# Clock-keeping products left out, projection units regrouped, and four weight splits moved from GpSimd to VectorE in an attention and two-layer kernel

## The chip, the cores and the metric

The kernel runs on one core of one Trainium2 chip. The metric is device time in microseconds, the median of several runs. The profile is one execution of the same program, with times counted from the start of its span. TensorE appears in it as PE (matmuls) and PEld (weight loads), VectorE as DVE, ScalarE as ACT, GpSimd as POOL and SyncE, which issues every transfer here, as SP.

## The reference, cut to what matters

```python
def sm_attn(qq, kk, vv):                     # softmax(scale * q k^T) v
    ...
p_packed = sm_attn(p, k, v)                  # 32 packed queries read 576 keys, per head
out = sm_attn(q, p_packed, p_packed)         # 576 queries read the 32 packed rows
x = out.transpose(0, 2, 1, 3).reshape(4608, 512)
xn = x / sqrt(mean(x * x) + 1e-6) * rms_g
g, val = xn @ w_gate, xn @ w_val             # 512 x 1536 each
x = (g * sigmoid(g) * val) @ w_out           # 1536 x 512
h = x @ w_in                                 # 512 x 2048
out = (h * cos(h)) @ w2_out                  # 2048 x 512
```

There are 8 batches with 8 heads of 64 columns, 576 tokens in each batch, float32 throughout. Some weights arrive in 64-bit form and are narrowed in the kernel (lines L134 to L150).

## The kernel before, in words

The program has four stretches, one behind the other.

**The prologue** (loop over `i`, 18 rounds, two to a batch) computes the packed attention for four heads at a time. A round transposes keys on PE (`u_kt`, tile `kp`, copied out by ACT as `kT`), multiplies packed queries with them (`u_s1`, tile `s`; the packed queries stand in a tile padded with zeros to 128 columns), takes the exponential on ACT (`u_e`), transposes it (`u_et`, tile `et`), and multiplies it with the values (`u_pp`, tile `pp`, 24 small products). Ahead of each group of transposes and of each third of the value products stands a call of `keep_hot`, one 128 x 288 product of a constant tile `hot` with itself, whose result is overwritten or not read. It has no use but to occupy PE. Along with this, rounds load and narrow the weights of the first layer (`w_prep`), and from round 4 on they do pieces of the second attention of batch 0 (`bg0_step`: tiles `qtp`, `sp`, `atp`, `xp`).

From round 10 on a round also does one or two **projection units** (`project`): the packed outputs times a block of the gate or value weights, four products into two PSUM tiles `mps`, which ACT and DVE copy out to `ev` (lines L528, L529); a store to DRAM is queued. In the prologue the tag `mm` has two PSUM buffers, so that a second unit, or a piece of attention with the same tag, has to wait until both copies of the unit before it have been made. The products `kp`, `et` and `pp` have a pool of four of their own.

**The joint stretch** (loop over `i`, 192 steps and two more) runs the first layer. In a step `gv_block` makes the gate and value products (two tiles of the tag `mm`, now of four buffers), ACT and DVE make `silu` of them (L701 to L703) and split it (`split_s`), and `acc_block` adds the output products of the step two before. Between them stand pieces of the next batch's attention (`att_step`). In eighteen of the steps 0 to 30 (`PJ_AT`) two projection units stand between `split_s` and `acc_block`. All engines run in the order in which the code is written (a manual schedule), and every engine takes its instructions in order.

**The last stretch** runs the second layer (`h_block`, `o_block`). Its order on each engine is made by the scheduler of the framework. Two of its blocks of input weights are split here, in `wm_split(b4)`: ACT rounds to the high part, and `tensor_tensor` on POOL makes the low part (`hilo`, L107 and L108).

Of the kernel before, what the change touches and what calls it, by code (L numbers as in the profile page):

```python
# [9 lines left out]
F32 = mybir.dt.float32  # L10
F32R = mybir.dt.float32r
I32 = mybir.dt.int32
AF = mybir.ActivationFunctionType
# [7 lines left out]
def kernel(  # L21
# [14 lines left out]
    nc = tc.nc  # L36
    B, H, S, D = q.shape
# [151 lines left out]
    pT = [u1.tile([128, 4, 160], F32, name=f"pT{i}") for i in range(2)]  # L189
    for t in pT:  # L190
        nc.gpsimd.memset(t, 0.0)
    hot = u1.tile([128, HALF], F32R, name="hot")
    nc.scalar.activation(out=hot, in_=ones[:, 0:1].to_broadcast([128, HALF]), func=AF.Copy)

    def keep_hot(ps, start=True):

        nc.tensor.matmul(ps, hot[:, :128], hot, start=start, stop=start)


    bq = a1.tile([128, H, 2 * NP], F32, name="bq")  # L200
    bdf = a1.tile([128, 2, 4, D], F32, name="bdf")
# [176 lines left out]
    def u_kt(i, hs):  # L378
        z = st[i]
        kT, kn = z["kT"], z["kn"]  # L380
        for h in hs:
            kp = ps_2.tile([128, HALF], F32, tag="kp", name="kp")
            keep_hot(kp)
            for c in range(CH):
                nc.tensor.transpose(
                    kp[:, c * CP:(c + 1) * CP], kn[:, h, 2 * c:2 * c + 2, :].rearrange("p c d -> p (c d)"),
                    ident[:CP, :CP],
                )
            nc.scalar.activation(out=kT[:, h], in_=kp, func=AF.Copy)
# [24 lines left out]
    def u_et(i):  # L414
        z = st[i]
        e = z["e"].rearrange("p a s -> p (a s)")
        eT = u2.tile([CP, NC_, 128], F32, tag="eT", name="eT", bufs=1)
        for hf in range(2):
            ep = ps_2.tile([128, CH, 128], F32, tag="kp", name="et")
            keep_hot(ep.rearrange("p c x -> p (c x)")[:, :HALF])  # L420
            et = ep[:CP]
            for c in range(CH):
                cc = hf * CH + c
                nc.tensor.transpose(et[:, c, :], e[:, cc * CP:(cc + 1) * CP], ident)
            nc.scalar.activation(out=eT[:, hf * CH:(hf + 1) * CH], in_=et, func=AF.Copy)
        z["eT"], mx = eT, z["mx"]
        nc.vector.tensor_scalar(out=mx[:, 2:3], in0=mx[:, 2:3], scalar1=1e-9, scalar2=None, op0=ALU.add)
        nc.vector.reciprocal(out=mx[:, 3:4], in_=mx[:, 2:3])

    def u_pp(i):  # L430
        b, g = divmod(i, 2)
        z = st[i]
        eT, vn, mx = z["eT"], nat_v.pop(i), z["mx"]
        pw = ps_2.tile([128, D + HALF], F32, tag="kp", name="pp")
        pp = pw[:, :D]
        for c in range(NC_):
            if c % 2 == 0:
                keep_hot(pw[:, D:], c == 0)
            for h in range(4):
                r = slice(h * NP, (h + 1) * NP)  # L440
                nc.tensor.matmul(
                    pp[r], eT[:, c, r], vn[:, h, c % CH * 2 + c // CH, :], start=c == 0, stop=c == NC_ - 1
                )
        cd = u2.tile([128, 2, D], F32, tag="cd", name="cd")
        nc.vector.tensor_scalar(
            out=cd, in0=pp.unsqueeze(1).to_broadcast([128, 2, D]), scalar1=mx[:, 3:4], scalar2=None, op0=ALU.mult
        )
        stores.append((c_dram[b][:, g, :], cd[:, 0, :]))
        z["cd"] = cd
# [109 lines left out]
    def wm_split(pool=wm_p):  # L559
        if not wm_q:  # L560
            return
        it = wm_q.pop(0)
        raw = wm_raw.pop(it)
        wm_t[it] = []
        for a in range(2):
            if it[0] == "w":
                t = pool.tile([128, 2, 4, 128], F32R, tag="wm", name="wmhl")
                src = raw[:, :, a * 128:(a + 1) * 128]
            else:
                t = pool.tile([128, 2, 2, 256], F32R, tag="wm", name="wmhl")  # L570
                src = raw.rearrange("p (k g) f -> p k g f", k=2)[:, :, a]
            on_pool = WM0_POOL if it[0] == 0 else True
            hilo(src, t[:, 0], t[:, 1], (nc.vector, nc.gpsimd)[on_pool])
            wm_t[it].append(t)

# [21 lines left out]
    for i in range(NG + 2):  # L597
        due = list(w_due(i))
        for n in due:
            w_load(n)  # L600
        load_k(i + 3)
        if i == 1:
            load_q()
            load_q()
        store(0)
        if i == U_ATT:
            att_load(0)
        if 0 < i <= NG:
            u_et(i - 1)
        if i < NG:  # L610
            u_s1(i)
        if i + 1 < NG:
            u_prep(i + 1)
            u_kt(i + 1, [0, 1])
        if 1 < i:
            u_fin(i - 2)
        if i < NG:
            u_e(i)
        if i + 1 < NG:
            u_kt(i + 1, [2, 3])  # L620
        for n in w_q:
            if n < W_KV:
                w_prep(n, 0)
        bg0_step(i, 1)
        for x in range(PJ_S.get(i, 0)):
            project(pj_0, 0)
            pj_0 += 1
        if 0 < i <= NG:
            u_pp(i - 1)
        for n in w_q:  # L630
            if n >= W_KV:
                w_prep(n, 0)
            w_prep(n, 1)
        w_q = due
        load_v(i + 2)
        if i in M0_S:
            wm_load((0, M0_S[i]))
        if i - 2 in M0_S:
            wm_split()
        bg0_step(i, 0 if i == U_ATT else 2 if i < 12 else 1)  # L640
# [168 lines left out]
    for i in range(len(seq) + LAG):  # L809
        b, hf, f = seq[min(i, len(seq) - 1)]  # L810
        j = i % B1
        if i < len(seq):
            if j == 0:
                if att is not None:
                    for _ in att:
                        pass
                att = attend(b + 1) if b + 1 < B else None
                att_done[0] = 0
                if b == B - 1:
                    ast.close()  # L820
                    rst.close()
                    bx["p"] = ctx.enter_context(tc.tile_pool(name="bx", bufs=2, side="right", reuse_waits="tile"))
            t = gv_block(b, hf, f)
            att_step(2 * i)
            split_s(b, hf, f, t)
            if i <= SPLIT0[-1] and i in SPLIT0:
                wm_split()
            store(0)
            for _ in range(PJ_AT.get(i, 0)):
                project(*PJ_L.pop(0))  # L830
            if i == LATE_AT:
                assert not PJ_L
                after_project()
        if i >= LAG:
            acc_block(*seq[i - LAG])
            att_step(2 * i + 1)
            b, hf, f = seq[i - LAG]
            if (b, hf) == (B - 1, 0):
                if f == BX:
                    load_x(0)  # L840
                if f in (BS, BS + 2):
                    split_x(0, (f - BS) // 2)
                if f >= BW and f < BW + 4:
                    w2_split(f - BW + NF1)
                if f >= BW - 2 and f < BW + 2:
                    w2_load(f - BW + 2 + NF1)
                if f >= NF1 - 2:
                    w2_load(f - NF1 + 2)
            if (b, hf) == (B - 1, 1):
                w2_split(f)  # L850
                if f + 2 < NF1:
                    w2_load(f + 2)
            b, hf, f = seq[min(i, len(seq) - 1)]
        n = W_B0 + i
        if W_B0 < n <= 4 * NCK:
            wy_prep(n - 1, 1)
        if n < 4 * NCK:
            wy_prep(n, 0)
            if n + 2 < 4 * NCK:
                wy_load(n + 2, wo_p[1], "wo")  # L860
        for n, (at, to) in WO_AT.items():
            if at == i:
                wo_load(n, *((wo_p[1], "wo")))
            if to == i:
                wo_prep(n, f1, 0)
            if to + 1 == i:
                wo_prep(n, None, 1)
            if to + 2 == i:
                wo_split(n)
        if j == AL_AT and b < B - 2:  # L870
            att_load(b + 2)
        if i > SPLIT0[-1] and b < B - 1 and hf == 1 and f % 2 == 1:
            wm_split()
        if i < len(seq) and b == B - 1 and j >= 11 and j % 2:
            if j < 23:
                wm_load(wm_next.pop(0))
            if j > 11:
                wm_split()
        if b < B - 1 and i in M_AT0 or b < B - 1 and i >= B1 and j in (M_AT if b > 1 else M_AT1):
            wm_load(wm_next.pop(0))  # L880
        if i >= W2_I0 and j in W2_AT:
            w2_fetch()
            w2_narrow(len(w2_items) > 0)
# [112 lines left out]
```

## Time and profile before

| | before |
|---|---|
| median of 3 runs | 1795.1 us (1792.65 to 1796.15) |
| the profiled execution | 1789.09 us, its span 1787.3 us |
| PE busy | 1725.5 us, 97% of the span |
| DVE, ACT, POOL busy | 1101.3, 863.8, 227.6 us |
| mean granted clock of TensorE | 0.976 of full speed |

PE is busy for nearly the whole of the span, but not equally: from about 340 us on it does not stop, and ahead of that it waits and runs at half its clock in places. A busy PE at half clock counts as busy, so the clock line of the page belongs beside the busy line.

### The profile page before, as it was taken

How to read it: one execution, taken by the hardware profiler on the slowest of the kernel's cores; microseconds unless marked ns; L12 is line 12 of the kernel's file. 1: busy time of each engine (PE TensorE's matmuls, PEld its weight loads, DVE VectorE, ACT ScalarE, POOL GpSimd, SP SyncE). 2: the span in 40 equal slices, each digit the busy share in tenths (PEclk: the TensorE clock that was granted, in tenths of full speed). 3: DMA queues.
4: the chain of work that ended last, by engine and by line, in shares of the span. 5: the costliest groups of instructions: out<-in, count | busy, mean ns of one | idle time of the engine just before them, and what ended most of it. 6: DMA issues, size and time to landing. Idle time of an engine off the chain costs nothing.

```text
span 1787.3 us, 28007 instructions
## 1 busy us (share of the span) xinstructions
PE 1725.5 (97%) x10992; PEld 1523.9 (85%) x10992; DVE 1101.3 (62%) x2108; ACT 863.8 (48%) x1662; POOL 227.6 (13%) x186
## 2 busy tenths in 40 slices
PE   7888798999999999999999999999999999999999
PEld 6666587899999999999999788888888888888887
DVE  2454378657686868686656656565656556565554
ACT  3443344445454545454545645454555545555444
POOL 1111142421111111212122200000000000000000
PEclk9888699999999999999999999999999999999999
DMA  9896375463443434342123301010101010000000
GB/s 224 214 233 188 110 251 173 144 214 103 141 140 105 148 103 144 107 147 80 67 73 122 106 1 47 1 48 1 47 1 47 13 36 24 25 0 24 1 24 24
DMA packets 114885, 165.41 MB, mean 93 GB/s; under 512 B 25152, under 2 KB 78400, under 8 KB 114752
## 3 DMA queue, kind: packets, MB, share of 16 engines
q1 hardware_dynamic: 114752, 163.61, 31.0%
q8 instruction: 86, 1.41, 0.3%
q14 instruction: 47, 0.39, 0.1%
HBM read 109.58 MB, written 54.00 MB: 92 GB/s over the span
## 4 chain that ended last, share of the span: by engine, by line
PE 84%; DVE 6%; DMA 4%; ACT 3%; issue 2%; POOL 1%; SPq 0%; DVEq 0%; ACTq 0%; POOLq 0%
PE ops L157 7%; PE ops L156 7%; PE ops L155 7%; PE hp L155 7%; PE hp L157 7%; PE hp L156 7%; PE acc L155 5%; PE acc L156 5%; PE acc L157 5%; PE gv L155 5%; PE gv L156 5%; PE gv L157 5%; PE mps L525 3%; DMA wraw<-in_moe_w_gate_dram 2%; PE sp L248 2%
## 5 line engine op out<-in xcount | busy, mean ns | idle before, releaser
L155 PE MATMUL gv<-apt,wmhl 128*128 128x288 f32 x768 | 233.4, 304 | 2.9 <-DVE silu L702 2.9
L155 PE MATMUL acc<-shl,wohl 128*128 128x288 f32 x768 | 236.2, 307 | 0.0
L156 PE MATMUL acc<-shl,wohl 128*128 128x288 f32 x768 | 228.9, 298 | 0.0
L155 PE MATMUL hp<-xhl,wmhl 128*128 128x512 f32 x576 | 225.0, 391 | 3.8 <-DVE r L916 3.8
L157 PE MATMUL acc<-shl,wohl 128*128 128x288 f32 x768 | 228.6, 298 | 0.0
L156 PE MATMUL gv<-apt,wmhl 128*128 128x288 f32 x768 | 227.3, 296 | 0.0
L157 PE MATMUL gv<-apt,wmhl 128*128 128x288 f32 x768 | 226.7, 295 | 0.0
L157 PE MATMUL hp<-xhl,wmhl 128*128 128x512 f32 x576 | 225.0, 391 | 0.0
L156 PE MATMUL hp<-xhl,wmhl 128*128 128x512 f32 x576 | 224.9, 390 | 0.0
L155 PE MATMUL ops<-w2hl,ghl 128*128 128x512 f32 x576 | 224.4, 390 | 0.0
L156 PE MATMUL ops<-w2hl,ghl 128*128 128x512 f32 x576 | 224.3, 389 | 0.0
L157 PE MATMUL ops<-w2hl,ghl 128*128 128x512 f32 x576 | 223.3, 390 | 0.0
L916 DVE TENSOR_TENSOR r<-r,hp 128x512 f32<-128x512 f32 x144 | 99.0, 688 | 188.6 <-ACT r L915 188.6
L108 POOL TENSOR_TENSOR wmhl<-wmraw,wmhl 128x512 fp32r<-128x512 f32 x112 | 145.0, 1316 | 537.6 <-ACT wmhl L107 530.0
L914 ACT ACTIVATE r<-r 128x512 f32<-128x512 f32 x144 | 91.0, 632 | 248.9 <-DVE r L913 248.9
L107 ACT ACTIVATE shl<-silu 128x288 fp32r<-128x288 f32 x192 | 85.3, 444 | 228.8 <-DVE silu L703 227.2
L909 ACT ACTIVATE kk<-hp,magic 128x512 f32<-128x512 f32 x144 | 99.3, 689 | 126.5 <-PE hp L157 126.5
L155 PEld LDWEIGHTS acc<-shl,wohl 128*128 128x128 f32 x768 | 145.7, 190 | 6.3 <-issue 6.3
L155 PEld LDWEIGHTS gv<-apt,wmhl 128*128 128x128 f32 x768 | 144.9, 189 | 4.3 <-DVE silu L702 4.0
L156 PEld LDWEIGHTS acc<-shl,wohl 128*128 128x128 f32 x768 | 146.1, 190 | 0.0
L157 PEld LDWEIGHTS acc<-shl,wohl 128*128 128x128 f32 x768 | 145.4, 189 | 0.0
L156 PEld LDWEIGHTS gv<-apt,wmhl 128*128 128x128 f32 x768 | 145.2, 189 | 0.0
(136 smaller groups left out, 3297.7 us busy)
## 6 DMA issues: line engine op xcount, KB each, us to landing
m<-ev SPq DMA_DIRECT2D x48, 512.0 KB
wmraw<-m SPq DMA_DIRECT2D x48, 512.0 KB
kn<-in_k_dram SPq DMA_DIRECT2D x16, 576.0 KB
vn<-in_v_dram SPq DMA_DIRECT2D x16, 576.0 KB
qnat<-in_q_dram SPq DMA_DIRECT2D x32, 288.0 KB
x_dram<-x SPq DMA_DIRECT2D x32, 288.0 KB
x1raw<-x_dram SPq DMA_DIRECT2D x18, 512.0 KB
raw<-in_moe_w_in_dram SPq DMA_DIRECT2D x16, 512.0 KB
```

Source lines behind the costliest of these rows:

```text
L107: nc.scalar.activation(out=hi, in_=src, func=AF.Copy)
L108: (eng or nc.vector).tensor_tensor(out=lo, in0=src, in1=hi.bitcast(F32), op=ALU.subtract)
L155: nc.tensor.matmul(ps, lhi, rhi, start=first, stop=False)
L156: nc.tensor.matmul(ps, lhi, rlo, start=False, stop=False)
L157: nc.tensor.matmul(ps, llo, rhi, start=False, stop=last)
L248: nc.tensor.matmul(sp[:, i, 2 * c:2 * c + 2, :], qT[:, i, c * CP:(c + 1) * CP], bq[:, 2 * j + i], start=True, stop=True,)
L525: nc.tensor.matmul(ps[r][:, j], ppT[bg][rows, 4 * kt + 2 * j + r], wy[rows, 2 * kt + j], start=True, stop=True)
L909: nc.scalar.activation(out=kk, in_=hp, func=AF.Identity, scale=1.0 / TWO_PI, bias=magic[:, 0:1])
L914: nc.scalar.activation(out=r, in_=r, func=AF.Abs)
L916: nc.vector.tensor_tensor(out=r, in0=r, in1=hp, op=ALU.mult)
```

## The change

It has four parts. The constant products and their tile go, 144 in number. In the prologue's rounds with two projection units the value products stand between the two units, no longer behind both. In the joint stretch the queued stores and the projection units stand behind the output products and the attention piece that follows these. And the two weight blocks that are split in the last stretch have their low parts made on DVE, not on POOL.

```diff
-    hot = u1.tile([128, HALF], F32R, name="hot")
-    nc.scalar.activation(out=hot, in_=ones[:, 0:1].to_broadcast([128, HALF]), func=AF.Copy)
-    def keep_hot(ps, start=True):
-        nc.tensor.matmul(ps, hot[:, :128], hot, start=start, stop=start)
...
             kp = ps_2.tile([128, HALF], F32, tag="kp", name="kp")
-            keep_hot(kp)
...
-            ep = ps_2.tile([128, CH, 128], F32, tag="kp", name="et")
-            keep_hot(ep.rearrange("p c x -> p (c x)")[:, :HALF])
-            et = ep[:CP]
+            et = ps_2.tile([CP, CH, 128], F32, tag="kp", name="et")
...
-        pw = ps_2.tile([128, D + HALF], F32, tag="kp", name="pp")
-        pp = pw[:, :D]
+        pp = ps_2.tile([128, D], F32, tag="kp", name="pp")
         for c in range(NC_):
-            if c % 2 == 0:
-                keep_hot(pw[:, D:], c == 0)
...
-            on_pool = WM0_POOL if it[0] == 0 else True
+            on_pool = pool is wm_p
...
         for x in range(PJ_S.get(i, 0)):
             project(pj_0, 0)
             pj_0 += 1
-        if 0 < i <= NG:
+            if x == 0 and 0 < i <= NG:
+                u_pp(i - 1)
+        if 0 < i <= NG and i not in PJ_S:
             u_pp(i - 1)
...
                 wm_split()
-            store(0)
-            for _ in range(PJ_AT.get(i, 0)):
-                project(*PJ_L.pop(0))
-            if i == LATE_AT:
-                assert not PJ_L
-                after_project()
         if i >= LAG:
             acc_block(*seq[i - LAG])
             att_step(2 * i + 1)
...
             b, hf, f = seq[min(i, len(seq) - 1)]
+        store(0)
+        for _ in range(PJ_AT.get(i, 0)):
+            project(*PJ_L.pop(0))
+        if i == LATE_AT:
+            assert not PJ_L
+            after_project()
```

On PE, in round 10 of the prologue, the two projection units (`mps`, four products each) stood together ahead of the value products (`pp`) before:

```order
L525 MATMUL mps<-wy,ppT_164 128x256 x8
L197 MATMUL pp<-hot 128x288
L441 MATMUL pp<-vn,eT 32x64 x8
L197 MATMUL pp<-hot 128x288
L441 MATMUL pp<-vn,eT 32x64 x8
L197 MATMUL pp<-hot 128x288
L441 MATMUL pp<-vn,eT 32x64 x8
L280 MATMUL atp<-ident,s 128x96 x3
L197 MATMUL et<-hot 128x288
L424 MATMUL et<-ident,e 96x128 x3
```

At the same place of the changed kernel PE has:

```order
L512 MATMUL mps<-wy,ppT_164 128x256 x4
L428 MATMUL pp<-vn,eT 32x64 x24
L512 MATMUL mps<-wy,ppT_164 128x256 x4
L273 MATMUL atp<-ident,s 128x96 x3
L414 MATMUL et<-ident,e 96x128 x6
```

The value products have moved between the units, and the attention transpose `atp`, which takes a buffer of the units' tag, now follows the second unit directly.

On PE, in step 2 of the joint stretch, the two units stood ahead of the twelve output products (`acc`) before:

```order
L157 MATMUL gv_2493<-apt,wmhl 128x288
L248 MATMUL sp<-bq,qT 96x64 x6
L238 MATMUL qtp<-ident,qnat 128x96 x3
L525 MATMUL mps<-wy,ppT_164 128x256 x8
L155 MATMUL acc<-shl,wohl 128x288
...
L157 MATMUL acc<-shl,wohl 128x288
L238 MATMUL qtp<-ident,qnat 128x96 x3
L155 MATMUL gv_2577<-apt,wmhl 128x288
```

In the changed kernel the same step reads:

```order
L157 MATMUL gv_2347<-apt,wmhl 128x288
L241 MATMUL sp<-bq,qT 96x64 x6
L231 MATMUL qtp<-ident,qnat 128x96 x3
L155 MATMUL acc<-shl,wohl 128x288
...
L157 MATMUL acc<-shl,wohl 128x288
L231 MATMUL qtp<-ident,qnat 128x96 x3
L512 MATMUL mps<-wy,ppT_164 128x256 x8
L155 MATMUL gv_2431<-apt,wmhl 128x288
```

The output products have come between the gate and value products and the units, and the next step's gate products follow the units directly.

On DVE, at the start of the last stretch, before (L910 to L916 are the elementwise work on the first blocks of `h`):

```order
L910 TENSOR_SCALAR kk<-kk 128x512
L912 SCALAR_TENSOR_TENSOR r<-kk,hp 128x512 x2
L913 SCALAR_TENSOR_TENSOR r<-kk,r 128x512 x2
L910 TENSOR_SCALAR kk<-kk 128x512
L912 SCALAR_TENSOR_TENSOR r<-kk,hp 128x512
L916 TENSOR_TENSOR r<-r,hp 128x512
```

In the changed kernel (where the same lines are L899 to L905):

```order
L899 TENSOR_SCALAR kk<-kk 128x512
L901 SCALAR_TENSOR_TENSOR r<-kk,hp 128x512 x2
L108 TENSOR_TENSOR wmhl<-wmraw,wmhl 128x512
L902 SCALAR_TENSOR_TENSOR r<-kk,r 128x512
L108 TENSOR_TENSOR wmhl<-wmraw,wmhl 128x512
L902 SCALAR_TENSOR_TENSOR r<-kk,r 128x512
L108 TENSOR_TENSOR wmhl<-wmraw,wmhl 128x512 x2
L899 TENSOR_SCALAR kk<-kk 128x512
L905 TENSOR_TENSOR r<-r,hp 128x512
```

The four splits that POOL made now stand in DVE's queue ahead of the first multiplication with `hp` (L905, L916 before), which frees the first PSUM tile of `h`.

## Rows read from the trace of the kernel before

**Rows 1.** The page: granted clock in 40 slices of 44.7 us, in tenths.

```profile
PEclk9888699999999999999999999999999999999999
```

**Rows 2.** Busy time by stretch: PE, PEld, DVE, ACT, POOL, clock, DMA share, GB/s.

```profile
0.00:104.00 104.00, 86.93 (x925) 67.35 (x925) 41.44 (x104) 43.49 (x112) 17.70 (x24) 0.93 0.98 226
104.00:226.00 122.00, 99.28 (x821) 70.99 (x820) 57.70 (x127) 46.45 (x107) 21.49 (x16) 0.76 0.59 167
226.00:340.00 114.00, 102.56 (x708) 89.13 (x707) 87.63 (x167) 57.41 (x120) 45.28 (x32) 0.96 0.61 197
340.00:1008.00 668.00, 661.92 (x5136) 655.70 (x5134) 458.39 (x967) 326.94 (x722) 143.12 (x114) 1.00 0.38 122
```

**Rows 3.** The chain of waits by line, 5 to 104 us, then 104 to 226 us.

```profile
by line: DMA wraw<-in_moe_w_gate_dram 33.6%; DMA wraw<-in_moe_w_val_dram 12.2%; DMA kn<-in_k_dram 10.6%; DMA q<-tf 8.3%; DMA vn<-in_v_dram 8.1%; PE s L398 4.3%; PE sp L248 3.0%; DMA bq<-q 2.8%; PE et L424 1.9%; ACT kT L389 1.4%; PE pp L441 
by line: PE mps L525 18.3%; issue 9.7%; PE pp L441 6.2%; PE pp L197 5.6%; DMA pn<-in_p_dram 3.9%; POOL ny L135 3.7%; PE s L398 3.6%; DVE s L326 2.8%; PE et L424 2.6%; ACT wy L134 2.4%; DVE mx L402 2.3%; PE atp L280 2.1%; ACT kT L389 2.1%; P
```

**Rows 4.** The constant products alone by stretch; columns PE, PEld, ACT, clock, DMA.

```profile
0.00:104.00 104.00, 36.12 (x88) 18.52 (x88) 0.44 (x1) 0.93 0.98 226
104.00:226.00 122.00, 26.65 (x57) 13.65 (x57) 0.00 (x0) 0.76 0.59 167
```

**Rows 5.** Timeline of PE in round 10: start, duration, instruction, idle time before.

```profile
110.85 1.14 PE L525 MATMUL mps<-wy,ppT 64*128 64x256 f32 x8
116.65 2.08 PE L525 MATMUL mps<-wy,ppT 64*128 64x256 f32 x8 [4.67 <-ACT ev L528]
118.66 0.61 PE L197 MATMUL pp<-hot 128*128 128x288 f32 x1
119.19 0.66 PE L441 MATMUL pp<-vn,eT 96*32 96x64 f32 x16
...
122.03 0.74 PE L280 MATMUL atp<-ident,s 96*128 96x96 f32 x3
```

**Rows 6.** Timeline of PE in round 12, at full clock.

```profile
150.35 1.13 PE L525 MATMUL mps<-wy,ppT 64*128 64x256 f32 x6 [0.57 <-ACT sq L308]
151.75 1.64 PE L525 MATMUL mps<-wy,ppT 64*128 64x256 f32 x8 [0.27 <-ACT ev L528]
153.32 0.40 PE L197 MATMUL pp<-hot 128*128 128x288 f32 x1
153.65 0.43 PE L441 MATMUL pp<-vn,eT 96*32 96x64 f32 x16
```

**Rows 7.** Busy time by stretch of 5 us, columns as in rows 2.

```profile
195.00:200.00 5.00, 0.89 (x4) 0.29 (x2) 3.89 (x10) 1.84 (x5) 0.24 (x1) 0.97 0.17 64
200.00:205.00 5.00, 3.77 (x28) 2.27 (x32) 0.90 (x3) 1.73 (x4) 0.00 (x0) 0.50 0.03 9
230.00:235.00 5.00, 2.94 (x23) 2.36 (x24) 4.76 (x10) 0.93 (x3) 1.92 (x2) 0.89 1.02 301
235.00:240.00 5.00, 5.00 (x21) 3.74 (x20) 3.73 (x8) 1.64 (x3) 0.00 (x0) 0.50 0.54 158
```

**Rows 8.** Waits of PE, 226 to 340 us: total, times, longest.

```profile
PE mps L525 <- DVE silu L702: 8.2, 6, 3.8
PE mps L525 <- ACT sq L308: 1.1, 1, 1.1
```

**Rows 9.** Timeline of PE around step 0 of the joint stretch.

```profile
224.10 2.00 PE L525 MATMUL mps<-wy,ppT 64*128 64x256 f32 x16
226.02 0.40 PE L155 MATMUL gv<-apt,wmhl 128*128 128x288 f32 x1
```

**Rows 10.** Start of the last stretch: timelines of POOL and DVE, PE's wait.

```profile
1001.25 6.09 POOL L108 TENSOR_TENSOR wmhl<-wmraw,wmhl 128x512 fp32r<-128x512 f32 x4 [6.61 <-ACT wmhl L107]
1001.38 3.42 DVE L913 SCALAR_TENSOR_TENSOR r<-kk,r 128x512 f32<-128x512 f32 x2
1008.14 0.68 DVE L913 SCALAR_TENSOR_TENSOR r<-kk,r 128x512 f32<-128x512 f32 x1
PE hp L155 <- DVE r L916: 3.8, 1, 3.8
```

## The prediction, made before the run

> **What bounds the kernel now.** I read the clock line first, then the stretches, then the chain of waits in each. The clock is at nine tenths or more everywhere but in slices 2 to 5 [rows 1]. By stretches, PE is busy for 661.92 of 668 us from 340 us on at clock 1.00, so whatever is saved or lost ahead of 340 us reaches the end one for one, as long as PE's work behind it stays the same; it does. Ahead of 340 us there are three cases [rows 2]. From 0 to 104 us the DMA engines are busy 0.98 of the time, and the chain runs over loads: the five DMA lines named sum to 72.8% of 99 us, the largest PE line is 4.3% [rows 3]. From 104 to 226 us DMA falls to 0.59, PE is busy 99.28 of 122 us at a mean clock of 0.76, and the chain is mixed: projection units 18.3%, value products 6.2%, constant products ahead of them 5.6%, the rest spread over DVE, ACT, POOL and issue [rows 3]. From 226 to 340 us PE idles 114 - 102.56 = 11.4 us, and DVE is busy 87.63 of 114 [rows 2].
>
> **Constant products out.** They are 144 matmuls, 88 of the recorded 145 records (one is cut by the border) ahead of 104 us and 57 behind [rows 4]. Ahead of 104 us I take 0: PE has work for less than the loads take, and what it saves it waits for the next load. Behind it, the cost on the path is bounded above by their busy time, 26.65 us [rows 4]; matmuls overlap, so the chain is nearer. There the ones ahead of value products hold 5.6% of 122 us = 6.8 us. Those ahead of keys and exponentials are not among the lines named, whose last full one has 2.1% = 2.6 us, so together they are between 0 and 5.2; I take 2.6. That is 9.4 us on the chain.
>
> **Value products between the units.** In round 10 PE stands 4.67 us between two units until ACT's copy, and the value products come only then: they hold 118.66 to 122.03, 3.37 us at half clock [rows 5]. Placed ahead of the second unit they run inside that wait. Three constant products of 119.19 - 118.66 = 0.53 us are counted already, which leaves 3.37 - 1.6 = 1.8 us. But what they covered is uncovered: the next piece of attention takes a buffer of the units and now waits for the copies of the second unit. That price is seen between two units at full clock: the first begins at 150.35, its six records of 2.0/16 us (at most, from the pair in [rows 9]) end near 151.1, the second begins at 151.75, so 0.65 us [rows 6]. Of the five rounds that change, four go on with such a piece and one (round 13) with the exponentials, which have buffers of their own. So the five give -1.8 in round 10, -0.65 in round 13, +0.65 in round 10 for the new wait, and nothing in the others, where one wait of this kind replaces another: -1.8.
>
> **The clock.** The constant products occupied PE, and PE's clock falls after it idles: 0.89 us of work in 195 to 200 us, at 0.97, is followed by 0.50 in the next 5 us [rows 7]. That fall came in spite of the constant products, since PE waited for another engine; so did the one in round 10, behind the 4.67 us. Without them PE's busy share falls a little in every stretch, so a few more such falls are to be expected, and those that end only when PE is busy last longer. A stretch of 5 us at half clock loses at most 2.5 us; PE is busy 99.28 of 122 us there [rows 2], so 2.0 is likelier; I take two more such stretches in the chain, +4. Bounds: 0 below (all falls come from waits that stay), and above all of PE's work in the chain of 104 to 226 us that runs at full clock today. Units and scores are 18.3% + 3.6% = 26.7 us of the chain, and at mean clock 0.76, thus 52% of the time at full, doubling that part adds 14 us.
>
> The Trainium skill speaks against this part: "TensorE: Matmul & The Clock Gate", Part 4, says that transposes on PE do not count as busy for the clock, and without constant products the rounds' transposes stand alone. By that rule the +4 would be nearer its upper bound, 14. No row of this trace shows a stretch of transposes alone.
>
> **Units behind the output products.** In 226 to 340 us units wait 8.2 us in six waits for DVE's L702 (the buffer of the same step's gate product) and 1.1 us for L308; PE idles 11.4 in all [rows 2, 8]. Twelve output products are ready all the while and stand behind. A step's twelve take 12 x 0.14 = 1.7 us, by the units' time for their columns (16 records of 256 columns in 2.0 us [rows 9], so 288 columns in 0.14). Put ahead, they fill up to 1.7 us of each wait. The longest, 3.8 us, stays with 2.1; the other waits on that row share 4.4 us, and I take them as filled: 11.4 - 2.1 = 9.3 us go. The fall of the clock at 235 us follows 2.94 us of work in 5 [rows 7]; with the products there it may not come, worth up to 2.5. New is that the next step's gate products follow the units directly and need their buffers. Steps 0 and 1 have no output products yet, and there the trace shows just this order: the pair takes 224.10 to 226.02, and the gate product starts at 226.02 without a wait [rows 9]. So I take 0.1 us in 18 steps, +1.8; upper bound 0.65 each [rows 6], 11.7. Sum -9.3 - 2.5 + 1.8 = -10.0.
>
> **What is late next.** DVE, at 77% in 226 to 340 us and 4.76 of 5 in 230 to 235 [rows 2, 7], also feeds the units' buffers, and in 104 to 226 us other engines hold most of the chain. So I let the savings pass to two thirds: (9.4 + 1.8) x 2/3 = 7.5 in the prologue, 10.0 x 2/3 = 6.7 in the joint stretch.
>
> **Last splits on DVE.** POOL's four take 6.09 us, and beside them two L913 on DVE take 3.42, while one alone takes 0.68: 2.06 us lost. PE then stands 3.8 us for L916, which is queued behind [rows 10]. On DVE four splits cost 4 x 0.68 = 2.7 (same size, L913's price), but in the new order only one and the first L913 stand ahead of the first activation. Loss and cost nearly cancel, the earlier activation gains some: I take -1.0, between +0.7 (all four ahead, 2.7 - 2.06) and -3.8 (the wait goes).
>
> The Trainium skill, "SBUF — State Buffer", Who interferes with whom, says that a DVE instruction with two SBUF inputs contends with a GpSimd instruction that reads SBUF. The trace agrees: 1.71 us each beside POOL, 0.68 without [rows 10].
>
> **Sum.** -7.5 + 4 - 6.7 - 1.0 = -11.2. The profiled execution's 1789.09 becomes 1778; it lies 6.0 below the median of the runs shown, 1795.1, so a median like that one becomes 1784. Within 0.2% is 3.6 us, about the width of the three runs and about what a measurement of this kernel can tell from no change.
>
> **Rivals.**
> *Clock lost in the prologue.* Constant products were what kept the clock, and without them the units, scores and transposes run at half. For it: 0.76 already with them. Against it: the falls follow waits of PE. Price +14 in 104 to 226 us, and in 5 to 104 us the scores and small products of the chain (4.3 + 3.0 + 1.9% of 99 = 9.1 us) double: +23 in place of +4. Then -11.2 + 19 = +8: 1803. It is measurably slower than before from a loss of 4 + 11.2 + 3.6 = 19 us on. Chance 0.10; a loss of about 14 us, with no measurable change near 1794, 0.12.
> *The units' new place gives nothing*, since gate products wait for copies instead (0.65 x 18 = 11.7 against 9.3 + 2.5). For it: DVE is at 77%. Against it: steps 0 and 1. Time 1784 + 6.7 = 1791. Chance 0.17.
> *More comes through*: savings in full, no lost clock, -9.4 - 1.8 - 10.0 - 3.8 = -25: 1770. Chance 0.13.
>
> **How the numbers follow.** The forecast, 1777 to 1789, has 0.48. Faster are it, the third rival and 0.13 of the second, which lies at the border: 0.74. The same is the rest of the second and the smaller loss of clock: 0.16. Slower is the larger loss: 0.10. The range 1769 to 1796 leaves out that loss and the edge of the fullest gain.
>
> **What would show it.** The units' waits for L702 should fall from 8.2 to under 3 us, with no gate wait for `ev` above 0.3. The first pair of units of the joint stretch (224.10 now [rows 9]) should start 2 to 6 us sooner; the loads up to 104 us should keep their times. DVE's L913 should take 0.7 each at the start of the last stretch, and PE's wait there shrink from 3.8. A mean clock under 0.70 in the prologue's second half would show the first rival.

## The result, and the profile after

The changed kernel takes 1766.84 us, the median of four runs (1763.76 to 1768.53), where the kernel before takes 1793.88 in four runs beside it: a ratio of 0.9849 with a 95% interval of 0.9827 to 0.9871. It is faster by 27 us. The forecast was 1784 and faster; the time lies 2 us below the range given, and close to the third rival ("More comes through", 1770), though with other shares of the parts than that rival has, so that the nearness is luck. A second group of runs gave the same kernel a ratio of 0.9869, 23 us (under Experiments).

The profiled execution took 1763.76 us with a span of 1761.9, and the mean granted clock is 0.973 (0.976 before). Where the time came from is read best from the starts of the same work in both executions:

| start on PE, us | before | after | earlier by |
|---|---|---|---|
| scores of round 10 | 106.4 | 99.8 | 6.6 |
| scores of round 15 | 191.8 | 175.9 | 15.9 |
| first output product of the joint stretch | 238.2 | 215.6 | 22.6 |
| output products of the 31st group | 405.5 | 381.0 | 24.4 |
| first product of the last stretch | 991.8 | 967.7 | 24.1 |
| end of the span | 1787.3 | 1761.9 | 25.4 |

So 22.6 of 25.4 us are there at the first output product, and from 405 to 991 us nothing is added or lost, as the 661.92 busy us of 668 in [rows 2] said. The clock line of the page, in 40 slices of 44.0 us, answers to [rows 1]:

```profile
PEclk9777799999999999999999999999999999999999
```

The lower clock stands in slices 2 to 5 as before, at 7, 7, 7, 7 in place of 8, 8, 8, 6. The same four stretches as in [rows 2], with the same columns (busy us of PE, PEld, DVE, ACT, POOL; clock, DMA share, GB/s):

```profile
0.00:104.00 104.00, 76.50 (x907) 58.76 (x909) 43.66 (x109) 46.17 (x118) 20.62 (x26) 0.87 1.00 238
104.00:226.00 122.00, 89.73 (x811) 68.51 (x810) 68.89 (x147) 50.30 (x116) 26.32 (x19) 0.76 0.66 193
226.00:340.00 114.00, 108.87 (x777) 98.27 (x776) 90.58 (x176) 61.23 (x127) 47.18 (x34) 0.97 0.60 195
340.00:1008.00 668.00, 662.85 (x5056) 652.56 (x5055) 462.29 (x967) 331.85 (x722) 128.97 (x104) 1.00 0.37 118
```

PE is busy less in the first two stretches, and in the second the clock is the 0.76 of before. In the third PE idles 114 - 108.87 = 5.1 us, where it was 11.4. The chain of waits from 5 to 104 us still runs over loads, five DMA lines with 83.9% where five had 72.8% in [rows 3]:

```profile
by line: DMA kn<-in_k_dram 36.0%; DMA q<-tf 17.4%; DMA wraw<-in_moe_w_val_dram 11.6%; DMA wraw<-in_moe_w_gate_dram 11.2%; DMA vn<-in_v_dram 7.7%; DMA bq<-q 2.7%; SPq L343 1.9%; issue 1.6%; POOL wy L135 1.5%; DVE wy L144 1.3%; PE sp L241 1.2
```

The timeline of PE answers to [rows 5] in round 10 and to [rows 9] at the first units of the joint stretch (start, duration, instruction, idle time before; L512 to L516 were L525 to L529, L428 was L441):

```profile
103.78 1.14 PE L512 MATMUL mps<-wy,ppT 64*128 64x256 f32 x8
109.52 1.50 PE L428 MATMUL pp<-vn,eT 96*32 96x64 f32 x48 [4.61 <-DVE pT L368]
111.83 2.08 PE L512 MATMUL mps<-wy,ppT 64*128 64x256 f32 x8 [0.80 <-ACT ev L515]
114.59 0.74 PE L273 MATMUL atp<-ident,s 96*128 96x96 f32 x3 [0.68 <-ACT ev L515]
...
207.53 2.62 PE L512 MATMUL mps<-wy,ppT 64*128 64x256 f32 x16
210.08 0.40 PE L155 MATMUL gv<-apt,wmhl 128*128 128x288 f32 x1
```

In round 10 the value products stand between the units, but they don't run inside the wait: they wait themselves, 4.61 us, for the copy of `pT` on DVE (L368), which frees one of the four buffers that `kp`, `et`, `pp`, `tp` and the transposed packed queries share. Behind them the second unit waits 0.80 and the attention transpose 0.68. The first pair of the joint stretch starts at 207.53, 16.6 us sooner than at 224.10, where 2 to 6 us were expected.

The waits of PE from 205 to 400 us answer to [rows 8] (total, times, longest; L691 was L702):

```profile
PE mps L512 <- DVE silu L691: 3.6, 3, 2.1
PE mps L512 <- ACT sq L301: 1.0, 1, 1.0
PE gv L155 <- ACT ev L515: 0.4, 1, 0.4
PE gv L155 <- DVE ev L516: 0.4, 1, 0.4
```

The units' wait for `silu` has fallen from 8.2 us in six to 3.6 in three, the longest from 3.8 to 2.1, and gate products now wait for the units' copies twice, 0.8 us in all. At the start of the last stretch the timeline of DVE answers to [rows 10] (L902 was L913, L905 was L916):

```profile
977.23 0.68 DVE L108 TENSOR_TENSOR wmhl<-wmraw,wmhl 128x512 fp32r<-128x512 f32 x1
977.83 0.68 DVE L902 SCALAR_TENSOR_TENSOR r<-kk,r 128x512 f32<-128x512 f32 x1
978.43 0.68 DVE L108 TENSOR_TENSOR wmhl<-wmraw,wmhl 128x512 fp32r<-128x512 f32 x1
979.03 0.68 DVE L902 SCALAR_TENSOR_TENSOR r<-kk,r 128x512 f32<-128x512 f32 x1
```

and the wait of PE there is

```profile
PE hp L155 <- DVE r L905: 2.2, 1, 2.2
```

where it was 3.8.

### The profile page after: what moved, and what is told of

Read it like the earlier page. It is cut to its first block, busy times and chain, and to the rows that moved or that the text cites. A ratio compares the mean times of both kernels' runs of the same rounds, so it can differ in the third digit from the quotient of the medians.

```text
span 1761.9 us, 27740 instructions
## 1 busy us (share of the span) xinstructions
PE 1687.3 (96%) x10848; PEld 1497.8 (85%) x10848; DVE 1102.7 (63%) x2112; ACT 863.5 (49%) x1661; POOL 223.1 (13%) x182
## 4 chain that ended last, share of the span: by engine, by line
PE 82%; DMA 7%; DVE 5%; ACT 3%; issue 1%; POOL 1%; SPq 1%; DVEq 0%; ACTq 0%; POOLq 0%
PE ops L157 7%; PE ops L155 7%; PE ops L156 7%; PE hp L155 7%; PE hp L156 7%; PE hp L157 7%; PE gv L155 5%; PE acc L155 5%; PE acc L156 5%; PE acc L157 5%; PE gv L156 5%; PE gv L157 5%; PE mps L512 3%; DMA kn<-in_k_dram 2%; PE sp L241 1%
## 5 line engine op out<-in xcount | busy, mean ns | idle before, releaser
L905 DVE TENSOR_TENSOR r<-r,hp 128x512 f32<-128x512 f32 x144 | 99.0, 687 | 187.0 <-ACT r L904 187.0
L108 POOL TENSOR_TENSOR wmhl<-wmraw,wmhl 128x512 fp32r<-128x512 f32 x108 | 139.1, 1309 | 530.3 <-ACT wmhl L107 518.5
L898 ACT ACTIVATE kk<-hp,magic 128x512 f32<-128x512 f32 x144 | 99.2, 689 | 125.5 <-PE hp L157 125.5
L155 PEld LDWEIGHTS gv<-apt,wmhl 128*128 128x128 f32 x768 | 145.2, 189 | 11.8 <-DVE silu L691 4.4
L156 PEld LDWEIGHTS gv<-apt,wmhl 128*128 128x128 f32 x768 | 145.7, 190 | 0.0
L157 PEld LDWEIGHTS gv<-apt,wmhl 128*128 128x128 f32 x768 | 145.4, 189 | 0.0
L156 PEld LDWEIGHTS acc<-shl,wohl 128*128 128x128 f32 x768 | 145.2, 189 | 0.0
L155 PEld LDWEIGHTS acc<-shl,wohl 128*128 128x128 f32 x768 | 144.9, 189 | 0.0
```

The source lines that it names most:

```text
L108: (eng or nc.vector).tensor_tensor(out=lo, in0=src, in1=hi.bitcast(F32), op=ALU.subtract)
L155: nc.tensor.matmul(ps, lhi, rhi, start=first, stop=False)
L156: nc.tensor.matmul(ps, lhi, rlo, start=False, stop=False)
L157: nc.tensor.matmul(ps, llo, rhi, start=False, stop=last)
L898: nc.scalar.activation(out=kk, in_=hp, func=AF.Identity, scale=1.0 / TWO_PI, bias=magic[:, 0:1])
L905: nc.vector.tensor_tensor(out=r, in0=r, in1=hp, op=ALU.mult)
```

## Experiments

The theory under test is the sum of the prediction: most of the gain should come from the units' new place and from a part of the constant products behind 104 us, some of it lost again to the clock. The rival after the result: the constant products cost their whole place in PE's queue, and the clock takes nothing back. Intervals are 95%; each group of runs stood beside its own runs of the kernel before (medians 1789.92, 1789.96 and 1789.78).

**The four parts alone.** Each kernel is the one before with one part of the change: constant products out; value products between the units; units and stores behind the output products; the last splits on DVE.

Constants out:

```diff
-            keep_hot(kp)
...
-            keep_hot(ep.rearrange("p c x -> p (c x)")[:, :HALF])
...
-                keep_hot(pw[:, D:], c == 0)
```

> The kernel before with the constant products alone left out. Theory A (they stood on the path in the whole prologue, the first 104 us too): 13 to 18 us faster, round 10 begins 5 to 7 us sooner. Theory B (the loads bound the first 104 us, and the early lead is the work of another part): 5 to 8 us faster, round 10 begins within 2 us of its old place. Rival of the prediction (the clock pays for it): no faster than 2 us, mean clock of 104 to 226 us under 0.70.

Measured: 1773.24 us, ratio 0.9911 [0.9891, 0.993], which is 0.0089 x 1790 = 15.9 us.

Value products between the units:

```diff
             pj_0 += 1
-        if 0 < i <= NG:
+            if x == 0 and 0 < i <= NG:
+                u_pp(i - 1)
+        if 0 < i <= NG and i not in PJ_S:
             u_pp(i - 1)
```

> The kernel before with the value products alone moved between the units. Theory A: within 3 us of before (the prediction's -1.8). Theory B, in which the moved values carry much of the gain of rounds 10 to 14: 5 to 9 us faster.

Measured: 1789.91 us, ratio 0.9994 [0.9983, 1.0006]: no change that can be told.

Units and stores behind the output products:

```diff
-            store(0)
-            for _ in range(PJ_AT.get(i, 0)):
-                project(*PJ_L.pop(0))
...
             b, hf, f = seq[min(i, len(seq) - 1)]
+        store(0)
+        for _ in range(PJ_AT.get(i, 0)):
+            project(*PJ_L.pop(0))
```

> The kernel before with stores and units alone moved behind the output products. Theory A: 7 to 10 us faster, since nearly the full -10.0 comes through and not two thirds. Rival: 3 us or less, because the joint stretch gains only when the prologue hands over sooner.

Measured: 1780.87 us, ratio 0.9952 [0.9939, 0.9966], 8.6 us.

The last splits on DVE:

```diff
-            on_pool = WM0_POOL if it[0] == 0 else True
+            on_pool = pool is wm_p
```

> The kernel before with the four last weight splits alone on DVE. Theory A: 1 to 2 us faster, PE's wait at the start of the last stretch 2 to 2.7 us in place of 3.8. Rival: no change that can be measured, PE's wait as before.

Measured: 1786.61 us, ratio 0.9986 [0.9975, 0.9998], 2.5 us.

The parts sum to 15.9 + 1.1 + 8.6 + 2.5 = 28 us and the whole gave 27, so they add up within their intervals (about 2 to 3.5 us either way each), and the constant products alone are over half of it.

**Constants by rounds.** Now `keep_hot` is left out in rounds 0 to 9 alone, in rounds 10 and later alone, or doubled in rounds 0 to 9. Round 10's scores start at 106.4 us before, so this divides the run about where the prediction did.

```diff
+    rnd = [0]
     def keep_hot(ps, start=True):
-        nc.tensor.matmul(ps, hot[:, :128], hot, start=start, stop=start)
+        if rnd[0] >= 10:
+            nc.tensor.matmul(ps, hot[:, :128], hot, start=start, stop=start)
...
+        rnd[0] = i
```

This is the first of the three, with the last line in the loop over the rounds. The second has `< 10`, and the third keeps the product and adds another one `if rnd[0] < 10`.

> The kernel before with the constant products left out in rounds 0 to 9 alone. Theory A (PE's work stands on the path there, because each round's loads are issued only when a round before it has released buffers and results): 5 to 8 us faster. Theory B (the loads bound those rounds): within 2 us of before, and round 10 begins where it did.

> The kernel before with the constant products left out from round 10 on alone. Theory A: 8 to 11 us faster, the rest of the 16 that all of them gave (9.4 us was their share of the chain). Theory B: 14 us or more.

> The kernel before with two constant products in place of one at each place in rounds 0 to 9. Theory A: 5 to 10 us slower, as much as leaving them out gains. Theory B: within 2 us of before.

Measured: out early 1786.89 us, 0.9979 [0.9967, 0.9992], 3.8 us; out late 1775.94 us, 0.9918 [0.9905, 0.993], 14.7 us; doubled early 1790.3 us, 1.0005 [0.9991, 1.0018], no change that can be told. So ahead of 104 us the constants are nearly free, and doubling them costs nothing that can be told; the gain sits behind. The 3.8 lies between what the two theories named (5 to 8, and within 2). 3.8 and 14.7 sum to 18.5, and both together gave 15.9, which the intervals allow.

The profiles show how it comes about. I take the same work in each, so that both ends are the same instructions: from the first scores to those of round 10, from those to the first output product, and from the first units of the joint stretch to the output products of its 31st group. In the kernel before these are (columns as in [rows 2]):

```profile
10.30:106.43 96.13, 85.71 (x950) 65.97 (x949) 41.50 (x104) 42.96 (x111) 16.19 (x11) 0.93 1.01 234
...
106.43:238.20 131.77, 106.69 (x840) 77.04 (x839) 66.36 (x142) 50.10 (x115) 24.64 (x19) 0.76 0.60 173
...
224.10:405.50 181.40, 169.96 (x1238) 153.05 (x1237) 127.33 (x248) 90.32 (x188) 63.24 (x46) 0.97 0.59 193
```

With the constants out late, the second of them is

```profile
106.80:223.24 116.44, 87.21 (x787) 64.26 (x786) 66.52 (x142) 49.55 (x116) 25.08 (x19) 0.79 0.67 196
```

It is 15.3 us shorter: PE's busy time falls by 106.69 - 87.21 = 19.5 us, and its idle time grows from 25.08 to 29.23 us, by 4.15. The constants' places in the queue, from the start of one to the start of PE's next instruction, sum to 18.0 us over the 53 records there (0.53 us at half clock in [rows 5], 0.33 at full in [rows 6]). So they account for the fall of the busy time but for 1.5 us, and the other engines took back a fifth of it as new waits. The kernel with all constants out has the same code from round 10 on, and its stretch is

```profile
98.82:218.35 119.53, 89.03 (x788) 65.68 (x787) 66.70 (x142) 50.86 (x118) 26.23 (x19) 0.77 0.64 189
```

12.2 us shorter than before, with 17.7 us less busy time and 5.4 us more idle time. So two executions of the same work differ by 3 us, and the new waits took back a fifth to a third. The mean granted clock is 0.79 and 0.77 in these two, where it is 0.76 before: worked out from that, PE ran at half clock for 2 x 0.24 x 131.77 = 63 us before and for 2 x 0.21 x 116.44 = 49 us with the constants out late. The groups by line of the same stretch (busy us, mean ns of one | idle us before them) say the same of the kernel before and the one with the constants out late; before:

```profile
L525 PE MATMUL mps<-wy,ppT 64*128 64x256 f32 x128 | 32.2, 528 | 15.1 <-ACT ev L528 5.3 <-DVE mx L427 3.8 <-DVE ahl L108 1.8
L398 PE MATMUL s<-kT,pT 64*128 64x288 f32 x96 | 14.7, 449 | 0.0
...
L197 PE MATMUL pp<-hot 128*128 128x288 f32 x21 | 10.9, 518 | 0.0
L385 PE MATMUL kp<-ident,kn 96*128 96x96 f32 x60 | 9.0, 263 | 0.0
```

and with the constants out late:

```profile
L528 PE MATMUL mps<-wy,ppT 64*128 64x256 f32 x128 | 30.9, 508 | 17.2 <-ACT ev L531 6.3 <-DVE mx L430 3.8 <-DVE ahl L108 2.7
L401 PE MATMUL s<-kT,pT 64*128 64x288 f32 x96 | 14.8, 453 | 0.0
...
L388 PE MATMUL kp<-ident,kn 96*128 96x96 f32 x60 | 8.3, 273 | 7.5 <-ACT eT L428 6.7 <-ACT kT L392 0.6
```

One unit product takes 508 ns instead of 528, one score product 453 instead of 449: what is left runs about as fast as before. The idle time ahead of the units grows by 2.1 us, and that ahead of the key transposes is 7.5 us, where the constants of `kp`, which stood there before, had 5.5 (a row that is not shown).

With the constants out early, the first of the three is

```profile
9.20:101.90 92.70, 71.77 (x865) 55.29 (x864) 41.20 (x104) 40.77 (x110) 14.89 (x11) 0.85 1.03 241
```

Here the busy time falls by 13.9 us and the idle time grows from 10.4 to 20.9, so 10.5 us are given back and 3.4 stay. The clock does fall here, from 0.93 to 0.85, and PE's busy time shrinks less than the constants' places, 23.7 us over 87 records. But the DMA engines are busy all the time, and the loss lies inside the wait for loads.

**Units, read in the profile.** The kernel with the units' new place alone has, from its first units of the joint stretch to the same output products,

```profile
221.94:395.90 173.96, 167.61 (x1237) 152.45 (x1237) 129.67 (x247) 91.02 (x188) 64.71 (x46) 0.97 0.60 199
```

7.4 us less than 181.40: idle time from 11.4 to 6.4 us, busy time 2.3 us less for the same products. The other 2.2 us of the profiled execution's lead were there at 221.94, in code that this part doesn't touch. The kernel with the splits alone, which has the code of before up to the last stretch, shows such a lead too in its profiled execution (3.0 us at the scores of round 6, 1.8 at those of round 15), so the 8.6 us of the timed runs may hold some of that.

**The splits, read in the profile.** With that part alone, PE's wait is the one of the whole change, line for line:

```profile
PE hp L155 <- DVE r L916: 2.2, 1, 2.2
```

**The whole change without the value products' new place.**

```diff
-            if x == 0 and 0 < i <= NG:
-                u_pp(i - 1)
-        if 0 < i <= NG and i not in PJ_S:
+        if 0 < i <= NG:
             u_pp(i - 1)
```

> The changed kernel with the value products back behind both units, the other three parts kept. If the new place of the values gives nothing (alone it gave a ratio of 0.9994): within 2 us of the changed kernel, a ratio to before of 0.983 to 0.987. If it pays only together with the other parts: 4 us or more slower than the changed kernel, a ratio of 0.987 or more.

Measured: 1763.33 us, 0.9841 [0.9824, 0.9859], against 0.9849 for the whole change. A second time, with the changed kernel itself beside it:

> The changed kernel unaltered, for comparison on one chip with the next two. All theories: a ratio to before of 0.983 to 0.987.

> The changed kernel with the value products back behind both units, again, beside the unaltered one. If the new place is worth nothing: within 2 us of the changed kernel. If it costs (the wait for the second unit's copies is then uncovered in four of five rounds, 0.7 us each): 2 to 4 us faster than the changed kernel.

Measured: 1766.33 us, 0.9869 [0.985, 0.9889] for the changed kernel, and 1764.89 us, 0.9857 [0.9839, 0.9875] without that part. The intervals don't separate the part from nothing, in either direction; both comparisons lie on the side on which the kernel is faster without it, by 1.4 and 2.1 us. The profiles say more. From round 10's scores to the first gate product of the joint stretch, the changed kernel of the second group and the one without that part have (columns as in [rows 2])

```profile
101.21:205.43 104.22, 73.01 (x698) 52.82 (x698) 54.98 (x120) 41.45 (x100) 21.67 (x16) 0.76 0.59 176
...
107.54:208.25 100.71, 75.11 (x699) 53.74 (x698) 54.85 (x120) 40.86 (x99) 21.40 (x16) 0.77 0.64 185
```

The three kept traces with the part and no constants need 104.2 to 104.6 us for this work, and the five without either (constants out, constants out late, the two runs of the changed kernel without the part, and the version beyond both) 99.2 to 102.3. With the constants in, the part alone needs 117.2 us, and five traces without it 113.0 to 115.3. So in these traces the new place costs 2 to 5 us, which the timed runs are too coarse to tell. It is idle time of PE, 31.2 us against 25.6 in the two rows. The largest waits with the part, and the two that only it has among the smaller ones, are (total, times, longest)

```profile
PE kp L377 <- ACT eT L415: 7.8, 1, 7.8
PE mps L512 <- DVE mx L417: 5.4, 1, 5.4
PE pp L428 <- DVE pT L368: 4.4, 1, 4.4
...
PE atp L273 <- ACT ev L515: 1.4, 2, 0.7
PE xp L155 <- ACT ev L515: 1.3, 2, 0.7
```

and without it

```profile
PE kp L377 <- ACT eT L415: 6.7, 1, 6.7
PE mps L512 <- ACT ev L515: 4.6, 3, 3.9
PE mps L512 <- DVE mx L417: 4.0, 1, 4.0
```

The wait of round 10 changes its name and not its length: what was put between the units could not start there. The four waits of attention pieces (`atp`, `xp`) for the second unit's copies are new, 2.7 us, and two later waits grow by 2.5.

**Transposes alone.** Ahead of the gate products of step 100 of the joint stretch, in the changed kernel, 120 transposes of the identity are added; their result is not read.

```diff
+            if i == 100:
+                tb = psb[0].tile([128, 128], F32, tag="mm", name="tburst")
+                for _ in range(120):
+                    nc.tensor.transpose(tb, ident, ident)
             t = gv_block(b, hf, f)
```

> The changed kernel with 120 transposes of the 128 x 128 identity put one behind the other ahead of step 100 of the joint stretch, where PE has been at full clock for over 200 us (extra work, its result not used). If transposes do not count as busy for the clock: the granted clock falls to 0.50 during or right behind the stretch of some 12 us, and a product of the step behind takes about twice its 0.30 us. If they count: no fall there, the clock stays at 1.00, and the kernel is longer by the transposes' own time alone, 12 to 14 us.

One execution took 1777.53 us, 11.2 more than the changed kernel's median in the same group, a little under the 12 to 14 expected. The timeline of PE there:

```profile
637.01 13.26 PE L815 MATMUL tburst<-ident 128*128 128x128 f32 x120
650.03 0.38 PE L155 MATMUL gv<-apt,wmhl 128*128 128x288 f32 x1
650.25 0.29 PE L156 MATMUL gv<-apt,wmhl 128*128 128x288 f32 x1
```

and the stretches of 5 us over it and behind it (clock is the number behind POOL's):

```profile
637.00:642.00 5.00, 5.00 (x49) 5.00 (x47) 2.24 (x4) 0.98 (x2) 0.00 (x0) 1.00 0.49 176
642.00:647.00 5.00, 5.00 (x48) 5.00 (x47) 0.00 (x0) 0.00 (x0) 0.00 (x0) 1.00 0.11 40
647.00:652.00 5.00, 5.00 (x47) 5.00 (x45) 0.38 (x1) 0.41 (x1) 0.00 (x0) 1.00 0.02 3
652.00:657.00 5.00, 5.00 (x44) 5.00 (x43) 2.47 (x7) 1.71 (x4) 0.00 (x0) 1.00 0.63 165
```

PE does nothing but transposes for 13 us, the granted clock stays at 1.00, and the gate products behind it take 0.38 and 0.29 us, no longer than the one at 210.08 in the changed kernel (0.40) and those that follow it there.

**A version beyond both.** POOL's narrowing (`ny L135`) stood on the chain from 104 to 226 us with 3.7% [rows 3]. Without the value products' new place, the last four blocks of output weights are narrowed on DVE:

```diff
-        narrow(wo_raw[f], wo_y[f], True, part)
+        narrow(wo_raw[f], wo_y[f], f >= WO_U, part)
```

> As the kernel before this one, and one step of narrowing the four output weight blocks of rounds 14 to 17 on DVE in place of POOL. If the rounds from 14 on are now bound by that chain over ACT, POOL and DVE (POOL's step takes 1.50 us, DVE's own steps of this size 0.43): 1 to 4 us faster than values_behind_again. If it is a load or a store that holds them: within 1 us of it.

Measured: 1762.1 us, 0.9845 [0.9823, 0.9867]. It is the lowest median of its group, but the interval overlaps those of the two kernels beside it; whether it beats the changed kernel stays open.

## Why the prediction missed

The forecast sum was -11.2 us and the runs gave -27.1, so 15.9 are missing (12 by the second group's 23). (The median of before fell from 1795.1 to 1793.88 with a fourth run, which is the other microsecond.) Term by term:

**Constants behind 104 us: the step that failed.** They were put at 9.4 us, their share of the chain of waits, of which two thirds should pass, 6.3. Measured are 14.7. The two thirds were a fair guess: of 19.5 us that PE's busy time shrank by, 15.3 came through, 79%, and 69% in the second trace. The chain's share was read rightly too: all lines of the constants on it from 104 to 226 us sum to 6.8 + 1.3 + 1.3 = 9.4 us. What failed is to take that share for the cost. The chain names the instruction that ended last at each step, and about half of the constants' places are on no line of it; still they cost. The likely reason, which no run isolates, is that PE takes its instructions in order and is busy 99.28 of 122 us [rows 2], so that each constant also delayed what other engines waited for. The size to take was the places in the queue, 18.0 us, which lies midway between the chain's share and the busy time that was named as the upper bound, 26.65.

**The clock: a loss was taken, and none came.** +4 was taken, between 0 and +14. Between round 10's scores and the first output product the mean granted clock is 0.79 and 0.77 in the two traces with the late constants out and the rest as before, and 0.76 before; what was left ran no slower. Together with the term above, that is the miss: -7.5 + 4 = -3.5 was forecast for constants and value products, and -15.9 - 1.1 = -17.0 measured with the parts alone, so 13.5 are missing there. The prediction's own argument against the rival, that falls follow waits of PE, fits that stretch: the waits stayed, and the time at half clock did not grow. The sign named for that rival, a mean clock under 0.70 in the prologue's second half, didn't come either: it is 0.76 in the changed kernel from 104 to 226 us. The fall that was feared came ahead of 104 us, 0.93 to 0.85, where the loads hide it.

A stretch of transposes alone was not to be found in the trace of before; the run that makes one shows 120 of them, 13.26 / 120 = 0.11 us apart, at a granted clock of 1.00, and 1.00 behind them. The Trainium skill, "TensorE: Matmul & The Clock Gate", Part 4, says that transposes do not count as busy in the way that other products do; by that rule the clock term would have been near +14. Here the trace does not agree with it, for float32 transposes in a row that start at full clock; whether transposes raise a low clock no run shows, and the prologue's are fewer and stand between waits.

**Constants ahead of 104 us: right within 4 us.** 0 was taken and 3.8 measured; doubling them cost nothing that can be told. "What it saves it waits for the next load" holds for 10.5 of 13.9 us. That the loads keep their times can't be read from one pair of traces, 226 against 238 GB/s and round 10 6.6 us sooner: round 10's scores start at 103.9 to 106.8 us in the five kept traces with single constants in the early rounds, and at 98.8 to 107.5 in the eight without. (With the constants doubled the one trace has 111.4, though the timed runs are no slower.)

**Value products between the units: small in time, and the step wrong.** -1.8 was taken and -1.1 measured, not different from 0; the traces show a cost of 2 to 5 us from round 10 on. That they run inside the wait failed, since they wait for DVE's `pT` themselves. In round 10 the new wait behind the second unit is 0.68 us, where 0.65 was taken. But that in the other rounds one wait replaces another failed too: three such waits of attention pieces, 0.7 us each, came on top there.

**Units behind the output products: right, a little small.** 6.7 was taken, 10.0 in full, and 8.6 measured (6.1 to 10.9 by the interval). The wait for L702 went to 3.6 and not below 3, the longest to 2.1 as worked out. The gate products' new waits are 0.8 us in all, less than the 1.8 taken, though two of them are 0.4 and not below 0.3. Idle time fell by 5.1 us and busy time by 2.3, near the 2.5 that one stretch less at half clock was put at; but the mean clock is 0.97 in both rows, so that the 2.3 are the clock's is not shown.

**Splits on DVE: right.** 1.0 was taken and 2.5 measured, 0.4 to 4.5 by the interval, so the two can't be told apart; L902 takes 0.68 us each without POOL beside it, where they took 1.71 beside it [rows 10], and the wait of 3.8 us went to 2.2, by 1.6. The 2.5 lies inside the bounds named, +0.7 to -3.8.

So constants, values and clock miss 13.5 us, the units 1.9 and the splits 1.5: 16.9, where 15.9 are to be explained, since the parts alone sum to 28.1 and the whole gave 27.1.

Only argued is why the waits behind 104 us took back so little: the DMA share is 0.59 there against 0.98 ahead [rows 2], which fits, but no run changed that alone. And the busy and idle times are those of one execution of each kernel. The time to round 10's scores varies most from one to the next: 99.75 and 107.54 us in the two traces of the changed kernel without the values' new place, which are the same program.

## What to carry to other kernels

Here work without use, on an engine that takes its instructions in order and was busy for four fifths of the time, cost its places in the queue, start to next start, less what reappeared as waits; its share of the chain of waits was too small. To price it, split the same piece of work, between the same two instructions, into busy and idle time, and ask of each stretch what would fill the gap: where loads were late the gap closed again (10.5 of 13.9 us), where engines were late it mostly did not (4.2 of 19.5). Moving work into a wait helps only if that work doesn't wait just as long itself, and what it covered at its old place has to be priced in every round.

## What the runs showed of the hardware

Products that were there to keep TensorE's clock up did not keep it up where it was low: 0.76 with them, and 0.77 and 0.79 without them, from round 10's scores to the first output product; ahead of that, where PE waits for loads, they did (0.93 against 0.85), at no gain in time. Transposes alone, 120 in 13.26 us, kept the granted clock at the 1.00 that it had before them. And the DMA share is no measure of what the loads could still take: in the first 104 us it is 0.98 at 226 GB/s before and 0.99 at 246 GB/s with all constants out.
